# Fewer filler matmuls, small turns taken together, the slots' sum one slot later, and a combine in even blocks

## The chip, the core and the metric

The kernel runs on one NeuronCore of a Trainium2 chip. TensorE (PE in the profile, its weight loads PEld) does the matmuls, VectorE (DVE), ScalarE (ACT) and GpSimd (POOL) the work between them, and SyncE's queue (SPq) issues every DMA. Each engine takes its instructions in the order in which they were written; an engine that waits holds up all that stands behind it. The metric is the time of one execution on the device, in microseconds (us), as a median over runs.

## What is computed

Two things in a row, cut here to what matters. First a recurrence over time with a decaying state, for 4 batches and 8 heads, 768 steps, 48 numbers per head:

```python
for t in range(S):
    cur = np.einsum('bhd,bhe->bhde', u[None] * kt, vt)
    y[:, :, t] = np.einsum('bhd,bhde->bhe', rt, state + cur)
    state = wt[:, :, :, None] * state + np.einsum('bhd,bhe->bhde', kt, vt)
```

Its output, x with 3072 rows (tokens) of 384, goes through a soft mixture of 8 experts with 4 slots each:

```python
logits = x @ phi
d = np.exp(logits - logits.max(0)); d /= d.sum(0)     # over the tokens
slot_input = d.T @ x                                  # 32 slots
slot_out[e] = np.maximum(slot_input[e] @ w1[e], 0.0) @ w2[e]
c = np.exp(logits - logits.max(1)); c /= c.sum(1)     # over the slots
return c @ slot_out
```

## The kernel before

The time axis is cut into 6 chunks of 128 steps. The main loop (L702) has 16 turns, n = 0 to 15, called slots here: slot n handles one pair of heads, and four of them (j = 0 to 3) make a batch. A seventeenth pass (n = 16) only ends the last pair. The order of all work is written by hand: nothing is moved by a scheduler, and every engine runs its part in the written order.

What a slot does, with the names that the change touches:

- DVE makes the running products of the decays for the packed inputs (units u, three per batch): `a_back` (L507) and `a_fwd` (L518) are scans over 774 columns, `a_k` (L515) and `a_r` (L524) multiply k and r by them. POOL makes the products r times k (`a_rk`, L502) in two buffers that alternate.
- PE turns k (`b_kn`, L538; ACT copies it out, L540 and L542), makes the chunk states (`b_u`, L571), the scores in two halves (`b_scores`, L549, into the two PSUM banks ap) and the bonus terms (`b_bonus`, L563, which read the buffer of `a_rk` and write the bank that the state scan reads).
- ACT copies each half of the scores out (`b_at`, L554) and POOL masks it (L556). DVE scans the states (`b_state`, L580). POOL multiplies v by the bonus (`b_av`, L596).
- One slot later PE adds up the result of the pair, `c_inter` (L605) and `c_av` (L614, its second half reads the second half of the masked scores), and `c_evac` takes it out of the two banks y: DVE for one head (L625), ACT and POOL for the other (L627, L628).
- Two slots later `l_turn` turns x (L73, into the banks y; ACT copies it out, L640), and `l_mm` (L77) multiplies by phi. One batch later the soft part follows: `s_max` and `s_exp` (L96), then in the slot j = 3 `s_dturn` (L103, ACT copy L105) and `s_rows` (L128, ACT copy L130), which share one bank tp[1] but use other columns of it, and `s_mm` (L110), the sum over tokens, into that bank too. `s_acc` (L122, L124) and `s_sum` take it out on DVE. `s_rows_exp` and `s_norm` make the weights for the combine.

`keep_warm` (L664) issues matmuls of a constant with 512 columns whose result nobody reads, called fillers here. The table `warm` (L666) says how many stand at five places of each of the first four slots.

After the loop the end starts at L831: the last turns and logits, the soft part of the last batch, `up_proj` (L186), `up_relu`, `turn`, then `down_proj` (L222) in three groups of output columns (160, 160 and 64). `mix` (L242) makes the combine c @ slot_out of one column group in blocks, four banks at a time, DVE and ACT copy them out (L247), and SP writes them (L249). It is a generator: `down_proj` calls its next step after each of its 8 inner rounds through the list `steps` (L904). The weights come by DMA throughout, 512 KB or 640 KB at a time.

Of the kernel before, what the change touches and what calls it, by code (L numbers as in the profile page):

```python
# [49 lines left out]
def rwkv_soft_moe(ctx: ExitStack, tc: tile.TileContext, wc, krc, vc, cst, w1, w2, out):  # L50
# [183 lines left out]
    def mix(cT, S4, cg, o, banks):  # L234
        lo, hi = COLS[cg]
        wd = hi - lo
        per = min(6, 512 // wd)
        for i0 in range(0, 6, per):
            ops = [banks[r][:, 0:per * wd].rearrange("p (i d) -> p i d", d=wd) for r in range(4)]
            for i in range(per):  # L240
                for r in range(4):
                    nc.tensor.matmul(out=ops[r][:, i, :], lhsT=cT[32 * r:32 * r + 32, i0 + i, :],  # L242
                                     rhs=S4[32 * r:32 * r + 32, lo:hi], start=True, stop=True)
            og = o[i0 // per][:, 0:4 * per * wd]
            for r in range(4):
                dst = og.rearrange("p (i r d) -> p i r d", r=4, d=wd)[:, :, r, :]
                (nc.vector.tensor_copy if r % 2 == 0 else nc.scalar.copy)(out=dst, in_=ops[r])  # L247
            yield
            nc.sync.dma_start(out=out[:, NT * lo + 4 * i0 * wd:NT * lo + 4 * (i0 + per) * wd],  # L249
                              in_=og)  # L250
# [379 lines left out]
    def l_turn(n, split=False):  # L630
        b, g = divmod(n, NG)
        kt = g - 1
        for t in range(C):
            l_turn_mm(xb[b % 2], t, kt, yb[t // 3][:, (t % 3) * P:(t % 3 + 1) * P])
        xT = xTs[kt % 2].rearrange("p (f c) t -> p f (c t)", f=2)
        if split:
            nc.scalar.copy(out=xT[:, 0], in_=yb[0][:, 0:384])
            nc.vector.tensor_copy(out=xT[:, 1], in_=yb[1][:, 0:384])
        else:
            nc.scalar.copy(out=xT, in_=ypp[:, :, 0:384])  # L640
# [25 lines left out]
    warm = {0: (0, 8, 8, 8, 8), 1: (4, 4, 4, 4, 4), 2: (4, 3, 3, 3, 3), 3: (2, 2, 2, 2, 2)}  # L666
# [23 lines left out]
    keep_warm(28, yb[0])  # L690
# [11 lines left out]
    for n in range(NIT + 1):  # L702
# [44 lines left out]
        if n == NIT:  # L747
            s_rows_exp(qs[b - 2])
            s_norm(b - 2, qs[b - 2])

        fill = warm.get(n, (0,) * 5)
        if live:
            keep_warm(fill[0], tp[1])
            b_kn(n)
        keep_warm(fill[1], yb[0])
# [4 lines left out]
        if live:  # L760
            b_u(n)
            keep_warm(fill[2], ap[0])
# [3 lines left out]
            b_bonus(n)  # L766
# [82 lines left out]
    s_acc(lb, q, sp)  # L849
    m_slots(q, yb[0][:, 0:KT * NS].rearrange("p (k s) -> p k s", s=NS))  # L850
# [47 lines left out]
    stage = [[wa[2], wa[3]], [wa[4], wa[5]], [wa[6]]]  # L898
# [5 lines left out]
    def steps(gen):  # L904
        return [lambda: next(gen, None)] * 7
# [92 lines left out]
```

## Time and profile before

| what | value |
|---|---|
| median of 3 runs | 235.68 us (233.25 to 236.63) |
| the profiled execution, its own time | 233.78 us |
| its span, first to last instruction | 232.1 us |
| mean granted clock of TensorE | 0.919 |
| instructions | 7909 |
| busy PE, DVE, POOL, ACT | 83%, 48%, 38%, 36% of the span |
| read from HBM, written | 44.44 MB, 4.72 MB |

The profiled execution took 1.9 us less than the median of the runs. The start of slot n is taken as the first L538 of that slot: slot 1 starts at 21.76, slot 4 at 49.12, slot 7 at 72.63, slot 8 at 85.95, slot 12 at 126.10 and slot 15 at 149.50 us. A row of the chain of waits or of the timeline has the start, the length, the engine and the line; in square brackets stands how long the engine had been idle and whose work ended that. A row of the windows view has a stretch, its length, the busy time of each engine with its number of instructions, and at its end the granted clock of TensorE, the share of DMA and its GB/s.

### The profile page before, as it was taken

How to read it: one execution, taken by the hardware profiler on the slowest of the kernel's cores; microseconds unless marked ns; L12 is line 12 of the kernel's file. 1: busy time of each engine (PE TensorE's matmuls, PEld its weight loads, DVE VectorE, ACT ScalarE, POOL GpSimd, SP SyncE). 2: the span in 40 equal slices, each digit the busy share in tenths (PEclk: the TensorE clock that was granted, in tenths of full speed). 3: DMA queues.
4: the chain of work that ended last, by engine and by line, in shares of the span. 5: the costliest groups of instructions: out<-in, count | busy, mean ns of one | idle time of the engine just before them, and what ended most of it. 6: DMA issues, size and time to landing. Idle time of an engine off the chain costs nothing.

```text
span 232.1 us, 7909 instructions
## 1 busy us (share of the span) xinstructions
PE 192.0 (83%) x3450; PEld 133.3 (57%) x3450; DVE 111.9 (48%) x181; ACT 84.1 (36%) x185; POOL 88.0 (38%) x130
## 2 busy tenths in 40 slices
PE   7999999988899589699858969968767987979620
PEld 2455866767787448668644867856323222757420
DVE  5888518537837648562765763423132141033410
ACT  3323233364467344435634537454120011112310
POOL 4347174385576354663645565537000000000000
PEclk9999999999999979959997999999765699999985
DMA  6987294996885895959089735993860089007470
GB/s 178 351 266 226 84 305 161 360 326 153 343 273 212 293 377 92 392 134 370 4 304 367 176 131 152 402 412 93 316 192 0 0 318 380 10 3 315 196 287 35
DMA packets 14922, 52.13 MB, mean 225 GB/s; under 512 B 1952, under 2 KB 2720, under 8 KB 14880
## 3 DMA queue, kind: packets, MB, share of 16 engines
q1 hardware_dynamic: 14880, 51.55, 63.6%
q8 instruction: 29, 0.48, 0.9%
q14 instruction: 13, 0.11, 0.2%
HBM read 44.44 MB, written 4.72 MB: 212 GB/s over the span
## 4 chain that ended last, share of the span: by engine, by line
PE 59%; DVE 15%; POOL 8%; ACT 5%; issue 4%; DMA 2%; SPq 1%; DVEq 0%; ACTq 0%; POOLq 0%
PE y L664 6%; PE G L186 6%; PE y L614 6%; PE ap L549 5%; PE y L222 5%; PE tp L563 4%; PE y L73 4%; PE tp L77 4%; PE tp L110 3%; POOL blkat L556 3%; POOL blka L502 3%; PE ap L664 3%; DVE Traw L580 2%; PE y L605 2%; DMA wa<-in_w_dram 2%
## 5 line engine op out<-in xcount | busy, mean ns | idle before, releaser
L556 POOL TENSOR_SCALAR_AFFINE_SELECT blkat<-blkat 128x768 f32<-128x768 f32 x32 | 27.6, 864 | 19.9 <-ACT blkat L554 17.1
L554 ACT COPY blkat<-ap 128x768 f32<-128x768 f32 x32 | 25.5, 798 | 23.5 <-PE ap L549 22.5
L614 PE MATMUL y<-v,blkat 128*64 128x48 f32 x768 | 27.2, 224 | 5.2 <-POOL blkat L556 5.2
L614 PEld LDWEIGHTS y<-v,blkat 128*64 128x64 f32 x768 | 24.3, 138 | 7.0 <-POOL blkat L556 6.1
L549 PE MATMUL ap<-krb 48*128 48x128 f32 x288 | 23.5, 297 | 0.0
L625 DVE TENSOR_TENSOR x<-y,av 128x288 f32<-128x288 f32 x17 | 7.7, 456 | 31.3 <-PE y L614 31.0
L628 POOL TENSOR_TENSOR x<-x,av 128x288 f32<-128x288 f32 x15 | 12.0, 801 | 27.9 <-ACT x L627 27.9
L507 DVE TENSOR_TENSOR_SCAN G<-blkw,G 128x774 f32<-128x774 f32 (+1 forms) x13 | 21.3, 1642 | 1.5 <-DMA blkw<-in_wc_dram 1.2
L549 PEld LDWEIGHTS ap<-krb 48*128 48x128 f32 x288 | 18.8, 195 | 5.4 <-issue 2.5
L518 DVE TENSOR_TENSOR_SCAN G<-blkw,G 128x774 f32<-128x774 f32 (+1 forms) x13 | 21.4, 1649 | 0.4
L664 PE MATMUL y<-siT 128*128 128x512 bf16 x62 | 17.3, 427 | 1.6 <-DVE siT L683 1.6
L515 DVE TENSOR_TENSOR krb<-krb,G 128x774 f32<-128x774 f32 (+1 forms) x13 | 11.6, 892 | 14.5 <-POOL blka L502 14.5
L502 POOL TENSOR_TENSOR blka<-krb 128x768 f32<-128x768 f32 x11 | 17.1, 1553 | 2.5 <-DMA krb<-in_krc_dram 2.5
L627 ACT COPY x<-y 128x288 f32<-128x288 f32 x15 | 6.0, 401 | 32.4 <-DVE x L625 32.4
L664 PEld LDWEIGHTS <-siT 128*128 128x128 bf16 x106 | 9.9, 103 | 13.1 <-issue 3.8
L186 PE MATMUL G<-wa,siT 128*32 128x512 f32 x96 | 13.9, 713 | 1.4 <-ACT x L194 1.1
L596 POOL TENSOR_TENSOR av<-v,asb 128x576 f32<-128x576 f32 x12 | 14.1, 1176 | 0.0
L580 DVE TENSOR_TENSOR_SCAN Traw<-tp,blkm 112x288 f32<-112x288 f32 x16 | 12.1, 754 | 3.0 <-PE tp L571 3.0
L73 PE MATMUL y<-cst,x 128*128 128x128 f32 x72 | 11.6, 303 | 1.7 <-DVE x L625 1.7
L222 PE MATMUL y<-wa,x 128*32 128x160 f32 (+1 forms) x144 | 12.2, 274 | 0.7 <-issue 0.7
L524 DVE TENSOR_TENSOR krb<-krb,G 128x774 f32<-128x774 f32 (+1 forms) x13 | 11.6, 892 | 0.8 <-POOL blka L502 0.5
L563 PE MATMUL tp<-cst,blka 128*64 128x4 f32 x288 | 11.0, 205 | 1.1 <-DVE Traw L580 0.7
(146 smaller groups left out, 337.5 us busy)
## 6 DMA issues: line engine op xcount, KB each, us to landing
wa<-in_w_dram SPq DMA_DIRECT2D x24, 512.0 KB, 7.0
krb<-in_krc_dram SPq DMA_DIRECT2D x11, 774.5 KB, 5.8
v<-in_vc_dram SPq DMA_DIRECT2D x16, 288.0 KB, 5.6
blkw<-in_wc_dram SPq DMA_DIRECT2D x11, 387.0 KB, 3.4
wa<-in_w_dram SPq DMA_DIRECT2D x6, 640.0 KB, 5.6
out_dram<-wa SPq DMA_DIRECT2D x4, 960.0 KB, 3.9
krb<-in_w_dram SPq DMA_DIRECT2D x4, 640.0 KB, 8.5
blka<-krb SPq DMA_DIRECT2D x24, 96.8 KB, 2.9
```

The source lines that it names most:

```text
L73: nc.tensor.transpose(out=tp, in_=x[:, t, kt * P:(kt + 1) * P], identity=ident)
L186: nc.tensor.matmul(out=hp[32 * g:32 * g + NS, :], lhsT=siT[:, e * KT + kt, :], rhs=wts[e][:, kt * F + hf * 512:kt * F + hf * 512 + 512], s ...
L222: nc.tensor.matmul(out=so[32 * g:32 * g + NS, :], lhsT=hT[ft // 2][:, ft % 2, e, :], rhs=wts[E + e][:, FT * lo + ft * wd:FT * lo + (ft + 1 ...
L502: nc.gpsimd.tensor_tensor(out=rks[u % 2][:, c0:c0 + cn_], in0=k3, in1=r3, op=ALU.mult)
L507: nc.vector.tensor_tensor_scan(out=G[:, lo:hi][:, ::-1], data0=w[:, lo:hi][:, ::-1], data1=g_one.broadcast_to([P, hi - lo]), initial=1.0, ...
L518: nc.vector.tensor_tensor_scan(out=G[:, lo:hi], data0=ws[u % 2][:, lo:hi], data1=g_zero.broadcast_to([P, hi - lo]), initial=1.0, op0=ALU.m ...
L549: nc.tensor.matmul(out=ap[h][:, cc * P:(cc + 1) * P], lhsT=kt[64 * h:64 * h + D, c * PIT + 1:c * PIT + PIT], rhs=rt[64 * h:64 * h + D, c * ...
L554: nc.scalar.copy(out=ats[n % 2][hf].rearrange("p h c t -> p h (c t)"), in_=app[:, :, 0:384])
L556: nc.gpsimd.affine_select(out=at, in_=at, pattern=[[0, 6], [1, P]], compare_op=ALU.is_gt, fill=0.0, base=0, channel_multiplier=-1)
L563: nc.tensor.matmul(out=aP[p:p + 64, c, :], lhsT=rks[(NU * b + g) % 2][:, c, p:p + 64], rhs=ub[:, g, :], start=True, stop=True)
L614: nc.tensor.matmul(out=yb[h][p:p + 64, c * D:(c + 1) * D], lhsT=ats[n % 2][c // 3][:, h, c % 3, p:p + 64], rhs=vt[:, c, h, :], start=False ...
L664: nc.tensor.matmul(out=bank[:, 0:512], lhsT=zb[:, 0:P], rhs=zb, start=True, stop=True)
```

## The change

1. The table `warm` is gone. Fillers are left only in slot 0 (4, 4 and 8, beside 24 in place of 28 at the very start); slots 1 to 3 have none. At the end, between the last turns, logits and sums, new fillers stand: 4, 5, 3 and 4, into the bank that `up_proj` uses later.
2. `s_turns` does the turns of `s_dturn` and `s_rows` one behind the other, four matmuls, and then the two ACT copies.
3. `s_mm`, `s_acc` and `s_sum` move from the end of slot j = 3 into the next slot, j = 0, ahead of the bonus. For batch 2, whose next slot is n = 16, they stand there at its start.
4. `b_bonus` moves behind `l_mm`, `s_mm` or `s_turns` of its slot.
5. `l_turn` moves behind the second half of the scores, and takes the bank pair as an argument. At n = 16 and in the end it uses ap, and it stands ahead of `c_inter` and `c_av` there.
6. `s_exp` stands behind the second half of the scores.
7. `mix` makes blocks of three row groups in all three column groups (the last was one block of six), issues the write as soon as a block's copies are written, and `steps` leaves two rounds of `down_proj` between the first and the second block.

Line numbers of the changed kernel are a little higher (`b_scores` is L559 there, `b_kn` L548, `c_inter` L615, `c_av` L624, `b_u` L581, `b_bonus` L573, `s_mm` L120, the fillers L674).

On PE, at the seam of slots 7 and 8, this stands in the row before (names: tp1 is the bank tp[1], ap and y the bank pairs, dT and dN the exponentials and their turn, blka and krb the packed inputs):

```order
L103 MATMUL tp1_80<-cst_61,dT_993 128x96 x2
L128 MATMUL tp1_80<-cst_61,lt_107 128x96 x2
L73 MATMUL y_81<-cst_61,x1_98 128x128 x6
L549 MATMUL ap_78<-blka_93 128x128 x6
L110 MATMUL tp1_80<-x0_97,dN_1090 32x384 x6
L538 MATMUL tp1_80<-cst_61,krb1_92 128x112 x4
L538 MATMUL tp0_79<-cst_61,krb1_92 128x112
L605 MATMUL y_81<-Tc1_106,blka_93 64x48 x20
L614 MATMUL y_81<-v1_100,blkat_94 64x48 x24
L571 MATMUL tp0_79<-v2_101,blkm_95 48x48 x10
L549 MATMUL ap_78<-krb1_92 128x128 x6
L563 MATMUL tp0_79<-cst_61,blka_93 64x4 x12
```

In the changed kernel PE has there:

```order
L109 MATMUL tp1_80<-cst_61,dT_935 128x96 x2
L111 MATMUL tp1_80<-cst_61,lt_107 128x96 x2
L559 MATMUL ap_78<-blka_93 128x128 x6
L73 MATMUL y_81<-cst_61,x1_98 128x128 x6
L548 MATMUL tp1_80<-cst_61,krb1_92 128x112 x4
L548 MATMUL tp0_79<-cst_61,krb1_92 128x112
L615 MATMUL y_81<-Tc1_106,blka_93 64x48 x20
L624 MATMUL y_81<-v1_100,blkat_94 64x48 x24
L581 MATMUL tp0_79<-v2_101,blkm_95 48x48 x10
L559 MATMUL ap_78<-krb1_92 128x128 x6
L120 MATMUL tp1_80<-x0_97,dN_1026 32x384 x6
L573 MATMUL tp0_79<-cst_61,blka_93 64x4 x12
```

The sum over tokens (L110, now L120) has moved from ahead of the turn of k to just ahead of the bonus, and the turn of x has changed places with the second half of the scores.

At the end of the loop, from slot 15's small turns on, PE has this in the row before:

```order
L103 MATMUL tp1_80<-cst_61,dT_1961 128x96 x2
L128 MATMUL tp1_80<-cst_61,lt_107 128x96 x2
L73 MATMUL y_81<-cst_61,x1_98 128x128 x6
L549 MATMUL ap_78<-blka_93 128x128 x6
L110 MATMUL tp1_80<-x0_97,dN_2051 32x384 x6
L605 MATMUL y_81<-Tc1_106,blka_93 64x48 x20
L614 MATMUL y_81<-v0_99,blkat_94 64x48 x24
L73 MATMUL y_81<-cst_61,x1_98 128x128 x6
L77 MATMUL tp1_80<-blkm_95,cst_61 32x256 x6
L73 MATMUL y_81<-cst_61,x1_98 128x128 x6
L77 MATMUL tp1_80<-blkm_95,cst_61 32x256 x3
L148 MATMUL tp0_79<-cst_61,nM_64 96x96
```

And this in the changed kernel, up to the first of the new fillers:

```order
L109 MATMUL tp1_80<-cst_61,dT_1903 128x96 x2
L111 MATMUL tp1_80<-cst_61,lt_107 128x96 x2
L559 MATMUL ap_78<-blka_93 128x128 x6
L73 MATMUL y_81<-cst_61,x1_98 128x128 x6
L120 MATMUL tp0_79<-x0_97,dN_1987 32x384 x6
L73 MATMUL ap_78<-cst_61,x1_98 128x128 x6
L77 MATMUL tp1_80<-blkm_95,cst_61 32x256 x3
L615 MATMUL y_81<-Tc1_106,blka_93 64x48 x20
L624 MATMUL y_81<-v0_99,blkat_94 64x48 x24
L77 MATMUL tp1_80<-blkm_95,cst_61 32x256 x3
L674 LDWEIGHTS siT_67
L674 MATMUL G_77<-siT_67 128x512
```

One turn of x and half of the first logits now stand ahead of the last pair's result, in other banks, and fillers behind it.

The diff, cut to its core:

```diff
+    def s_turns(q, dp, ln):
+        for n in range(2):
+            nc.tensor.transpose(out=dp[:, n, 0:TG], in_=q["dT"][:, n, :], identity=ident[0:TG, 0:TG])
+        for n in range(2):
+            nc.tensor.transpose(out=ln[:, n, 0:TG], in_=q["lt"][:, n, :], identity=ident[0:TG, 0:TG])
+        q["dN"] = small.tile([P, 2, TG], F32, name="dN", bufs=1)
+        nc.scalar.copy(out=q["dN"], in_=dp[:, :, 0:TG])
+        q["ce"] = ce = small.tile([P, 2 * NTG, NS], F32, name="ce", bufs=1)
+        nc.scalar.copy(out=ce.rearrange("p (n j) s -> p n (j s)", n=2), in_=ln[:, :, 0:TG])
...
     def mix(cT, S4, cg, o, banks):
-        per = min(6, 512 // wd)
+        per = 3
         for i0 in range(0, 6, per):
-            ops = [banks[r][:, 0:per * wd].rearrange("p (i d) -> p i d", d=wd) for r in range(4)]
+            off = i0 * wd if 6 * wd <= 512 else 0
+            ops = [banks[r][:, off:off + per * wd].rearrange("p (i d) -> p i d", d=wd) for r in range(4)]
...
+            nc.sync.dma_start(out=out[:, NT * lo + 4 * i0 * wd:NT * lo + 4 * (i0 + per) * wd], in_=og)
             yield
-            nc.sync.dma_start(out=out[:, NT * lo + 4 * i0 * wd:NT * lo + 4 * (i0 + per) * wd],
-                              in_=og)
...
-    warm = {0: (0, 8, 8, 8, 8), 1: (4, 4, 4, 4, 4), 2: (4, 3, 3, 3, 3), 3: (2, 2, 2, 2, 2)}
...
-    keep_warm(28, yb[0])
+    keep_warm(24, yb[0])
...
         if n == NIT:
-            s_rows_exp(qs[b - 2])
-            s_norm(b - 2, qs[b - 2])
+            q = qs[b - 2]
+            sp0 = tp[0][0:TG, 0:DM]
+            s_mm(xb[b % 2], q, sp0)
+            l_turn(l, app)
+            l_mm(0, xTs[0], lpv, True, False)
+            s_acc(b - 2, q, sp0)
+            s_sum(b - 2, q)
+            s_rows_exp(q)
+            s_norm(b - 2, q)
...
         if live:
             b_u(n)
-            keep_warm(fill[2], ap[0])
+            if n == 0:
+                keep_warm(4, ap[0])
             b_scores(n, 0)
             b_at(n, 0)
             b_state(n)
-            b_bonus(n)
+        if j == 0 and b > 1 and live:
+            q = qs[b - 2]
+            s_mm(xb[b % 2], q, spv)
+            s_acc(b - 2, q, spv)
+            s_sum(b - 2, q)
...
         if soft and j == 3:
-            q = qs[sb_]
-            s_dturn(q, dpv)
-            s_rows(q, lnv)
+            s_turns(qs[sb_], dpv, lnv)
+        if live:
+            b_bonus(n)
...
-        keep_warm(fill[3], yb[1])
-        if l >= 0 and lj >= 1:
-            l_turn(l)
+        if live:
+            if n == 0:
+                keep_warm(4, ap[0])
+            b_scores(n, 1)
+            b_at(n, 1)
+            if n == 0:
+                keep_warm(8, yb[0])
+        if l >= 0 and lj >= 1 and live:
+            l_turn(l, ypp)
         if soft and j == 2:
             s_exp(sb_, q)
-        if live:
-            keep_warm(fill[4], ap[0])
-            b_scores(n, 1)
-            b_at(n, 1)
-        if soft and j == 3:
-            s_mm(xb[sb_ % 2], q, spv)
-            s_acc(sb_, q, spv)
-            s_sum(sb_, q)
...
-    l_mm(0, xTs[0], lpv, True, False)
+    warm_bank = Gp[:, 0:512]
     l_mm(1, xTs[1], lpv, False, False)
-    l_turn(NIT - 1, split=True)
+    keep_warm(4, warm_bank)
+    l_turn(NIT - 1, app, split=True)
+    keep_warm(5, warm_bank)
     l_mm(2, xTs[0], lpv, False, True)
+    keep_warm(3, warm_bank)
...
     s_acc(lb, q, sp)
+    keep_warm(4, warm_bank)
...
     def steps(gen):
-        return [lambda: next(gen, None)] * 7
+        return [lambda: next(gen, None), lambda: None, lambda: None, lambda: next(gen, None)]
```

More of the change, by code (lines that the diff above doesn't have):

```diff
@@ L628, in c_evac, with l_turn @@
                 nc.gpsimd.tensor_tensor(out=xh, in0=xh, in1=avs[n % 2][:, h], op=ALU.add)
-    def l_turn(n, split=False):
+    def l_turn(n, pp, split=False):
         b, g = divmod(n, NG)
@@ L633, in l_turn @@
         for t in range(C):
-            l_turn_mm(xb[b % 2], t, kt, yb[t // 3][:, (t % 3) * P:(t % 3 + 1) * P])
+            l_turn_mm(xb[b % 2], t, kt, pp[:, t // 3, (t % 3) * P:(t % 3 + 1) * P])
         xT = xTs[kt % 2].rearrange("p (f c) t -> p f (c t)", f=2)
         if split:
-            nc.scalar.copy(out=xT[:, 0], in_=yb[0][:, 0:384])
-            nc.vector.tensor_copy(out=xT[:, 1], in_=yb[1][:, 0:384])
+            nc.scalar.copy(out=xT[:, 0], in_=pp[:, 0, 0:384])
+            nc.vector.tensor_copy(out=xT[:, 1], in_=pp[:, 1, 0:384])
         else:
-            nc.scalar.copy(out=xT, in_=ypp[:, :, 0:384])
+            nc.scalar.copy(out=xT, in_=pp[:, :, 0:384])
     lpv = tp[1][0:TG, 0:2 * P].rearrange("p (n q) -> p n q", n=2)
@@ L747, in rwkv_soft_moe @@
         if n == NIT:
-            s_rows_exp(qs[b - 2])
-            s_norm(b - 2, qs[b - 2])
-        fill = warm.get(n, (0,) * 5)
+            q = qs[b - 2]
[7 more added lines that the diff above has]
+            s_norm(b - 2, q)
         if live:
-            keep_warm(fill[0], tp[1])
             b_kn(n)
-        keep_warm(fill[1], yb[0])
         if m >= 0:
@@ L803, in rwkv_soft_moe @@
             b_av(n)
-        keep_warm(fill[3], yb[1])
-        if l >= 0 and lj >= 1:
-            l_turn(l)
+        if live:
[7 more added lines that the diff above has]
+            l_turn(l, ypp)
         if soft and j == 2:
             s_exp(sb_, q)
-        if live:
-            keep_warm(fill[4], ap[0])
-            b_scores(n, 1)
-            b_at(n, 1)
-        if soft and j == 3:
-            s_mm(xb[sb_ % 2], q, spv)
-            s_acc(sb_, q, spv)
-            s_sum(sb_, q)
-        if j == 0 and 1 < b < B + 1 and live:
+        if j == 0 and 1 < b and live:
             s_rows_exp(qs[b - 2], nc.gpsimd)
-        if j == 1 and 1 < b < B + 1 and live:
+        if j == 1 and 1 < b:
             s_norm(b - 2, qs[b - 2], nc.gpsimd)
@@ L897, in rwkv_soft_moe @@
     mb = [ap[0], ap[1], tp[0], tp[1]]
-    stage = [[wa[2], wa[3]], [wa[4], wa[5]], [wa[6]]]
+    stage = [[wa[2], wa[3]], [wa[4], wa[5]], [wa[6], wa[7]]]
     def fin(cg):
```

## The prediction, made before the changed kernel ran

> **What bounds the kernel now.** I read the granted clock by slices, the chain of waits in order of time, then the stretches by slot. The clock first, in 40 slices of 5.8 us: low digits stand in the loop (slices 15, 18 and 22) and for some 20 us at its end.
>
> ```profile
> PEclk9999999999999979959997999999765699999985
> ```
>
> The chain runs through PE's fillers (L664) until slot 3. The windows view of L664 alone gives PE's busy time and the number of fillers; then three places of the chain.
>
> ```profile
> 10.30:21.70 11.40, 8.23 (x36) 3.28 (x36) 1.00 0.76 227
> 21.70:32.10 10.40, 5.03 (x22) 1.71 (x20) 1.00 0.56 178
> 32.10:41.50 9.40, 3.91 (x15) 1.03 (x14) 1.00 0.61 230
> 41.50:49.10 7.60, 2.57 (x9) 0.62 (x8) 1.00 1.01 387
> ...
> 18.36 1.73 PE ap L664 x8
> 24.00 1.53 PE y L614 x48
> 52.05 0.91 PE y L614 x24
> ```
>
> Eight fillers take 1.73 us: 0.216 each, and they stand on PE between real work. From slot 4 on there are none. There the chain goes from the bonus on PE through POOL back to PE, and at the seam of slots 7 and 8 through DVE, ACT and the small turns:
>
> ```profile
> 71.89 0.43 DVE lt L773
> ...
> 78.39 0.47 DVE x L625
> 79.17 0.80 ACT blkat L554
> 80.25 0.38 PE tp L128 x2
> 80.64 0.66 PE y L73 x6
> 81.29 1.25 PE ap L549 x12
> 82.54 2.71 PE tp L110 x12
> 85.34 0.55 DVE SI L122
> 85.97 0.68 PE tp L538 x5
> ...
> 90.30 0.87 PE tp L563 x24
> 91.16 0.82 PE y L73 x6
> 92.04 1.55 POOL blka L502
> 93.85 1.13 POOL av L596
> 94.98 0.82 POOL blkat L556
> ```
>
> After the loop PE is the chain, half of the time at half clock:
>
> ```profile
> 158.17 1.48 PE tp L110 x12
> 162.73 0.83 DVE x L625 x2
> 163.60 1.54 PE y L73 x6
> 165.14 1.96 PE tp L77 x12
> 169.12 0.67 PE tp L77 x6
> 172.26 2.78 PE ap L110 x12
> 178.50 5.35 PE G L186 x24
> 184.26 3.57 PE G L186 x32
> ```
>
> The same 12 rows of L110 took 1.48 us at 158 and 2.78 at 172. 24 rows of L186 took 5.35, and the next 32 only 3.57.
>
> **The change, part by part.** The sum is made against the profiled execution, 233.78 us (span 232.1 and 1.7 around it).
>
> *Fillers of slots 0 to 3.* In slot 0 the result of the pair cannot come as early as PE could start it. POOL holds the mask of the second half (L556) behind `a_rk` of unit 2, which waited for its DMA, and `b_av`:
>
> ```profile
> 18.77 1.55 POOL L502 TENSOR_TENSOR blka<-krb 128x768 f32<-128x768 f32 x1 [0.90 <-DMA krb<-in_krc_dram]
> 20.54 1.18 POOL L596 TENSOR_TENSOR av<-v,asb 128x576 f32<-128x576 f32 x1
> 21.88 0.86 POOL L556 TENSOR_SCALAR_AFFINE_SELECT blkat<-blkat 128x768 f32<-128x768 f32 x1 [0.16 <-ACT blkat L554]
> ```
>
> That DMA's issue does not move. So the mask comes right behind L596, ends at 22.6, and the first c_av ends half its length (0.75) later, at 23.35 instead of 24.00 + 1.53 = 25.53: 2.2 gained, with fewer fillers or many. From there to 52.05, where the second half of slot 4's c_av starts, PE now has 38 fillers, counted in the written order (12 of slot 1 behind its c_av, 16 of slot 2, 10 of slot 3). At 0.216 they are 8.2. The waits that come up in their place, by the same rows: in slot 2 the POOL chain of 1.55 + 1.13 + 0.82 from the bonus to c_av's second half is longer than PE's work beside it by 1.3, and in slot 3 DVE's two scans push L625, and so ACT's copy and the scores, 1.0 late. So 2.2 + 8.2 - 2.3 and 0.4 for a shorter wait ahead of 52.05: **-8.5**. Ends: -10.4 with no new wait, and -2 if POOL and DMA hold slots 1 to 3 where they are.
>
> *Clock in the loop.* It falls without any long gap. In slot 9 the window below has PE busy 1.84 of 3.41 us, its gaps under 1 us each, and behind it the slot's mean is 0.74; slot 9 takes 12.9 us, its twin slot 13 at full clock 10.0. So one fall costs up to 2.9.
>
> ```profile
> 95.28:98.69 3.41, 1.84 (x50) 1.67 (x52) 1.74 (x3) 1.69 (x5) 1.54 (x3) 1.00 1.01 394
> ...
> 92.80:105.70 12.90, 11.09 (x181) 8.66 (x179) 7.28 (x10) 5.05 (x12) 8.12 (x12) 0.74 0.80 278
> 132.90:142.90 10.00, 8.15 (x181) 6.57 (x179) 5.91 (x8) 4.84 (x12) 6.31 (x11) 1.00 0.39 115
> ```
>
> In the changed kernel c_av's second half in slot 1 waits for that mask while PE has nothing else for some 2.8 us; with half a chance of a fall there (+1.45) and half a chance that slot 9's goes (-1.45) the likeliest net is **0**, between -2.9 and +5.8 (two falls more). The Trainium skill's page "TensorE: Matmul & The Clock Gate" (HAM oscillation) lets the clock fall only for an idle gap over about 3.4 us. By that rule slot 1 would not fall and slot 9's fall would be none; the window above disagrees, and the measurement decides. With the rule the sum would be 1.45 lower.
>
> *Seam of slots 7 and 8, and of 11 and 12.* The turn L128 waited for ACT's copy of L103's result, and ACT stood behind L554, L625 and so DVE's chain from 71.89. Now four matmuls go in one piece, but the second scores still need L554, so PE's wait shrinks and does not vanish. `l_mm` ahead of the bonus brings the start of DVE's chain 0.87 earlier (the bonus's length). So L554 ends at 79.97 - 0.87 = 79.1; scores 0.87 (L549 at full clock, the length that L563 has too), turn of x 0.82, and L538 starts at 80.8 instead of 85.97: -5.15. L110 comes back in slot 8, 1.48, and the wait for the mask there, 0.5. One more DMA, queue or POOL instruction is not issued. DVE's SI copy (0.55) now stands ahead of a later scan, which POOL's L502 holds anyway. Net -3.1, twice: **-6.2**. Ends: -7.4 (the waits in slots 9 and 13 shrink too) and 0 (rival 2).
>
> *Slot 15 to the logits.* One turn and half of the first logits go ahead of c_inter, where PE waited for L554 and for dN. Then L625 x2 still ends at 163.56; behind it came 1.54, 1.96, a turn and an evacuation until L77 at 169.12. Now the turn of the last pair alone stands behind it: 163.6, 0.5 of the four fillers in the way, 0.8 for the turn, 1.27 for its evacuation by ACT and then DVE, L77 at 166.2: **-2.9**. Ends -3.4 and -1.5 (if half clock stays).
>
> *Fillers at the end.* 4, 5, 3 and 4 lie where PE waits for L625, the evacuation, nM and SI; 16 x 0.216 = 3.5 fit in the waits but for those 0.5. What they are worth is the clock: L110 2.78 to 1.48, 24 rows of L186 from 5.35 to 24 x 3.57 / 32 = 2.68, small matmuls about 1.2: **-5.2**. Ends: -5.2 and 0.
>
> *Combine.* PE waits 0.98 ahead of the second block of the first group; two rounds of `down_proj` (8 rows each at 0.036, from 112 rows in 4.01) fill 0.58 of it. In the second group DVE's copies bind the next step: nothing. The last group in two blocks writes twice 384 KB for once 768 KB; the second block's matmuls wait for the first's copies in the same banks, so the last issue comes some 0.45 later, and the last write has half the bytes.
>
> ```profile
> 199.12 4.01 PE y L222 x112
> ...
> 208.80 0.41 PE L242 MATMUL ap<-x,blkw 32*128 32x160 f32 x2 [0.98 <-ACT wa L247]
> ...
> out_dram<-wa SPq DMA_DIRECT2D x4, 960.0 KB, 3.9
> ...
> out_dram<-wa SPq DMA_DIRECT2D x1, 768.0 KB, 5.3
> ```
>
> Its landing lies between half of 5.3 and the 3.9 of a larger write: 3.7 taken, so -1.6 + 0.45. Together **-1.8**; ends -2.8 and +0.5.
>
> Sum: -8.5 + 0 - 6.2 - 2.9 - 5.2 - 1.8 = -24.6, so 233.78 - 24.6 = 209.2. The median of the runs lies 1.9 above the profiled execution; with less than half of that added I forecast **210.0 us**.
>
> **Rivals.**
> 1. *The fillers at the end do not hold the clock.* For it: between them stand turns and waits, and windows only a little over half busy fell before. Against: in 163 to 173 PE would be busy over 70%. Then the last -5.2 goes, and 210.0 becomes 215.2. By the same clock page of the Trainium skill (Part 4, PE-mode transpose) turns do not count as activity, which makes this likelier; no run here shows it.
> 2. *POOL takes the loop's gain.* The bonus now comes 1.48 later in j = 0 and some 1.0 later in j = 1; `a_rk` (L502) waits for it, and c_av's second half waits for the 3.5 us of POOL behind it, where PE's work beside it is now 0.8 shorter (the turn or the sum that stood there). If that binds everywhere, the -6.2 goes: 216.2. Against: 91.98 to 95.80 was bound by it before, so part is paid already.
> 3. *Both*: 221.4.
> 4. *Slower: the clock stays low in the loop.* One mechanism: slots 1 to 3 without fillers start at half clock, and the loop, whose short matmuls hardly count, does not bring it back. Each slot so costs up to 2.9; from (24.6 + 4.7) / 2.9 = 10 slots on it is slower by over 2%; with all 15, 210.0 + 43.5 = 253. Against: slot 10 ran at full clock again behind slot 9's fall, with no filler near.
> 5. *The early gain is given back to DMA*: loads wait on DVE's scans, not on PE, and slots 1 to 3 keep their length but for 2: 216.5.
>
> **How the numbers follow.** My forecast 0.56, rival 1 0.16, rival 2 0.10, both 0.05, rival 5 0.08, rival 4 0.02, and 0.03 for mishaps within 2%. About 2% of this kernel's time, 4.7 us, is what a measurement can tell from no change. All but rival 4 and the last lie below 231: faster 0.95, same 0.03, slower 0.02. The forecast's own ends, with the clock's -2.9, the seams' -1.2 and the combine's -1.0, reach down to 205; upward rivals 1, 2 and 5 reach 216.5 and both 221.4. I take 203 to 220.
>
> **What would show it.** Slot 4's c_av second half near 43.5 instead of 52.05; slot 8's start some 5 earlier against slot 7's; L110 in slot 8 at 1.5; granted clock 1.00 from the logits through L186, its first 24 rows in about 2.7; a last write under 4. Slots 1 to 3 with the clock at 0.5, L186 still at 5.35 or c_av's second half waiting over 1 us in slots 5, 6, 9 and 10 would make the forecast wrong.

## The result, and the profile after

| | before | changed |
|---|---|---|
| median of the runs | 234.47 us (231.16 to 236.63, 4 runs) | 214.74 us (213.28 to 224.57, 4 runs) |
| the profiled execution | 233.78 us, span 232.1 | 215.24 us, span 213.5 |
| mean granted clock in it | 0.919 | 0.922 |

The ratio is 0.9227, with a 95% interval from 0.9086 to 0.9367: faster by 6 to 9%. 210.0 had been forecast, 4.7 less than was measured; 214.74 lies in the range. One of the four executions of the changed kernel, the one of 224.57, was granted a mean clock of 0.862, the other three 0.908 to 0.922.

The granted clock by slices of the changed kernel. The end is now at full clock but for the last slice; the low digits stand early, in slices 5 to 7, 11, 12 and 16.

```profile
PEclk9999655999559996999999999999999999999995
```

The windows view cut at the places of which the prediction speaks: slots 0 to 3, slots 4 to 14, slot 15 to the last logits (the last L77), from there to `up_proj`, its first 24 rows, and the rest. First the kernel before, then the changed one. The last three numbers are the granted clock, the share of DMA and GB/s.

```profile
10.07:49.12 39.05, 38.92 (x617) 25.95 (x615) 23.36 (x25) 13.92 (x29) 18.65 (x28) 1.00 0.72 247
49.12:149.50 100.38, 86.57 (x1860) 69.29 (x1858) 61.46 (x79) 49.84 (x108) 57.42 (x81) 0.93 0.72 244
149.50:169.12 19.62, 14.72 (x273) 10.41 (x272) 5.74 (x15) 7.80 (x17) 7.23 (x10) 0.91 0.77 283
169.12:178.50 9.38, 6.69 (x30) 3.27 (x31) 2.67 (x11) 1.51 (x6) 0.00 (x0) 0.57 0.31 95
178.50:183.85 5.35, 5.35 (x25) 1.06 (x26) 0.06 (x1) 0.00 (x0) 0.00 (x0) 0.50 0.00 0
183.85:232.10 48.25, 31.30 (x624) 19.89 (x624) 11.70 (x37) 7.89 (x20) 0.00 (x0) 0.92 0.48 186
```

```profile
8.91:46.11 37.20, 30.93 (x553) 26.16 (x554) 24.42 (x27) 14.25 (x30) 18.65 (x28) 0.82 0.70 238
46.11:142.62 96.51, 85.22 (x1859) 72.32 (x1857) 61.90 (x80) 50.33 (x109) 57.41 (x81) 0.93 0.79 264
142.62:158.62 16.00, 14.92 (x282) 10.70 (x281) 5.00 (x13) 7.82 (x17) 7.33 (x10) 1.00 0.80 290
158.62:165.62 7.00, 5.70 (x37) 2.48 (x38) 2.67 (x11) 1.51 (x6) 0.00 (x0) 1.00 0.75 297
165.62:168.40 2.78, 2.78 (x25) 0.74 (x26) 0.06 (x1) 0.00 (x0) 0.00 (x0) 1.00 0.02 6
168.40:213.50 45.10, 31.65 (x625) 20.15 (x624) 11.91 (x39) 8.12 (x22) 0.00 (x0) 0.93 0.51 198
```

Slots 0 to 3 lost 64 instructions of PE and 8.0 us of its busy time, but only 1.85 us of length: the clock there went from 1.00 to 0.82. The 96.51 of slots 4 to 14 are 3.87 less than before at the same mean clock. From slot 15 on every stretch came out about as forecast or shorter. The six differences and the first slot's earlier start (1.16) make the 18.6 by which the spans differ: 1.16 + 1.85 + 3.87 + 3.62 + 2.38 + 2.57 + 3.15.

What PE waited for between 30 and 140 us (us in total, times, the longest), first in the kernel before, then in the changed one:

```profile
PE tp L128 <- ACT dN L105: 5.1, 2, 2.6
PE y L614 <- POOL blkat L556: 4.1, 6, 1.1
```

```profile
PE ap L559 <- ACT blkat L564: 3.9, 4, 1.8
PE y L615 <- ACT blkm L650: 3.6, 8, 0.6
```

The wait for `dN` in the kernel before is its wait at the seams. In the changed kernel the wait there stands ahead of the second scores (first line); the prediction expected it to shrink and not to vanish. The wait for POOL's mask, 4.1 before, is down to 0.2. The wait of L615 is new, and no term had it: the turn of x now stands right ahead of the next slot's `c_inter` (L615), which writes the same two banks y, so PE waits there for ACT's copy of the turn (L650).

### The profile page after: what moved, and what is told of

Its sections match the earlier page's. It is cut to its first block, busy times and chain, and to the rows that moved or that the text cites. A ratio compares the mean times of both kernels' runs of the same rounds, so it can differ in the third digit from the quotient of the medians.

```text
span 213.5 us, 7814 instructions
## 1 busy us (share of the span) xinstructions
PE 178.5 (84%) x3397; PEld 135.5 (63%) x3400; DVE 111.6 (52%) x183; ACT 84.5 (40%) x187; POOL 88.1 (41%) x130
## 4 chain that ended last, share of the span: by engine, by line
PE 54%; DVE 14%; POOL 10%; ACT 7%; DMA 6%; issue 5%; SPq 1%; ACTq 0%; DVEq 0%; POOLq 0%
PE ap L559 10%; PE y L624 9%; DMA krb<-in_krc_dram 6%; PE G L196 5%; PE y L232 5%; DVE G L517 4%; PE y L615 4%; PE tp L581 3%; PE tp L77 3%; POOL blkat L566 3%; POOL av L606 3%; POOL blka L512 3%; PE tp L573 3%; ACT blkat L564 2%; DVE G L528 2%
## 5 line engine op out<-in xcount | busy, mean ns | idle before, releaser
L624 PE MATMUL y<-v,blkat 128*64 128x48 f32 x768 | 30.0, 238 | 4.1 <-POOL blkat L566 3.7
L564 ACT COPY blkat<-ap 128x768 f32<-128x768 f32 x32 | 25.6, 800 | 19.0 <-PE ap L559 17.7
L624 PEld LDWEIGHTS y<-v,blkat 128*64 128x64 f32 x768 | 27.2, 151 | 5.7 <-POOL blkat L566 4.2
L559 PE MATMUL ap<-krb 48*128 48x128 f32 x288 | 25.8, 315 | 1.1 <-issue 1.0
L559 PEld LDWEIGHTS ap<-krb 48*128 48x128 f32 x288 | 20.7, 210 | 3.1 <-issue 2.0
L517 DVE TENSOR_TENSOR_SCAN G<-blkw,G 128x774 f32<-128x774 f32 (+1 forms) x13 | 21.4, 1643 | 1.6 <-DMA blkw<-in_wc_dram 1.3
L525 DVE TENSOR_TENSOR krb<-krb,G 128x774 f32<-128x774 f32 (+1 forms) x13 | 11.6, 891 | 12.6 <-POOL blka L512 12.6
L573 PEld LDWEIGHTS tp<-cst,blka 128*64 128x64 f32 x288 | 10.2, 145 | 6.8 <-issue 5.0
L581 PE MATMUL tp<-v,blkm 128*48 128x48 f32 x320 | 11.2, 222 | 2.6 <-ACT blkm L552 2.6
L573 PE MATMUL tp<-cst,blka 128*64 128x4 f32 x288 | 11.2, 205 | 2.4 <-DVE Traw L590 1.4
L615 PE MATMUL y<-Tc,krb 48*64 48x48 f32 x480 | 10.6, 236 | 2.4 <-ACT blkm L650 2.4
L196 PE MATMUL G<-wa,siT 128*32 128x512 f32 x96 | 11.3, 597 | 1.4 <-ACT x L204 1.1
L615 PEld LDWEIGHTS y<-Tc,krb 48*64 48x64 f32 x480 | 9.1, 148 | 4.8 <-ACT blkm L650 3.8
```

Source lines behind the costliest of these rows:

```text
L196: nc.tensor.matmul(out=hp[32 * g:32 * g + NS, :], lhsT=siT[:, e * KT + kt, :], rhs=wts[e][:, kt * F + hf * 512:kt * F + hf * 512 + 512], s ...
L517: nc.vector.tensor_tensor_scan(out=G[:, lo:hi][:, ::-1], data0=w[:, lo:hi][:, ::-1], data1=g_one.broadcast_to([P, hi - lo]), initial=1.0, ...
L559: nc.tensor.matmul(out=ap[h][:, cc * P:(cc + 1) * P], lhsT=kt[64 * h:64 * h + D, c * PIT + 1:c * PIT + PIT], rhs=rt[64 * h:64 * h + D, c * ...
L564: nc.scalar.copy(out=ats[n % 2][hf].rearrange("p h c t -> p h (c t)"), in_=app[:, :, 0:384])
L573: nc.tensor.matmul(out=aP[p:p + 64, c, :], lhsT=rks[(NU * b + g) % 2][:, c, p:p + 64], rhs=ub[:, g, :], start=True, stop=True)
L615: nc.tensor.matmul(out=yb[h][p:p + 64, c * D:(c + 1) * D], lhsT=rt[64 * h:64 * h + D, c * PIT + p:c * PIT + p + 64], rhs=T[64 * h:64 * h + ...
```

## The experiments

Four kernels ran beside each other in each of three groups, each group on one chip with its own runs of the kernel before. A time follows the clock that its execution was granted: of the kernel before, one with a mean clock of 0.836 took 246.59 us and one at 0.945 took 227.88. So medians are compared inside a group, and stretches at clock 1.00 with each other.

### Fillers in the wait of slot 1

```diff
-    def c_av(n):
+    def c_av(n, fill=0):
...
         for c in range(C):
+            if c == 3 and fill:
+                keep_warm(fill, ap[0])
...
-            c_av(m)
+            c_av(m, 15 if n == 1 else 0)
```

> The changed kernel with 15 more fillers in slot 1, between the two halves of c_av, where PE waited 3.48 us for POOL's mask; they cost 15 x 0.216 = 3.2 us inside that wait, so nothing. Theory 1 (slots 1 to 3 lose to the clock what the missing fillers give): the granted clock stays 1.00 from 23 to 37 us, slot 4 starts near 42 instead of 46.1, and the time falls from 214.7 by 3 to 6, to 209 to 212. Rival (the new order holds slots 1 to 6 up, not the clock): the clock stays up, slot 7 starts within 1.5 us of its 74.4, and the time is 213 to 216.

211.73 us (208.52 to 215.65, 4 runs), ratio 0.9137 [0.884, 0.9434]. First what happens there in the changed kernel, from its chain of waits (start, length, work): the load of `krb` lands late, POOL takes its steps, and PE comes out of the wait of 3.48 us at half clock: 1.52 for 24 rows that take 0.91 at full clock.

```profile
10.38 9.13 DMA krb<-in_krc_dram
...
19.67 1.55 POOL blka L512
...
21.48 1.13 POOL av L606
22.61 0.82 POOL blkat L566
...
23.48 1.52 PE y L624 x24
```

With the fillers (timeline of PE):

```profile
19.84 3.41 PE L676 MATMUL ap<-siT 128*128 128x512 bf16 x14
23.19 0.91 PE L626 MATMUL y<-v,blkat 128*64 128x48 f32 x24
...
31.07 0.91 PE L626 MATMUL y<-v,blkat 128*64 128x48 f32 x24 [1.57 <-POOL blkat L566]
...
32.35 1.23 PE L559 MATMUL ap<-krb 48*128 48x128 f32 x12
```

The fall behind slot 1's wait is gone (0.91), and the next wait, 1.57 us in slot 2, has one behind it (1.23 for 12 rows that take 0.94 at full clock). One covered wait hands the fall on to the next: slot 4 starts at 46.18, where the changed kernel had 46.11 and theory 1 had put it near 42. Two limits of this run: its load landed earlier, so the mask was ready at 21.97, and the fillers, which end at 23.25, held c_av's second half up by 1.2 us. And the interval of its ratio covers that of the changed kernel, 0.9227, so no difference in time is shown.

### The turn of x ahead of the second scores again

```diff
+        if l >= 0 and lj >= 1 and live:
+            l_turn(l, ypp)
         if live:
             b_scores(n, 1)
             b_at(n, 1)
-        if l >= 0 and lj >= 1 and live:
-            l_turn(l, ypp)
```

> The changed kernel with the turn of x ahead of the second scores again, as before the change, and all else kept. Theory (the moved turn made a wait of its own: c_inter writes the banks y, which ACT's copy of the turn L650 still reads, 0.3 to 0.65 us in 8 slots): those waits go, second scores and masks come 0.8 later where POOL has the time, 214.7 falls by 1 to 3 us. Rival (the earlier mask is worth as much): c_av's second half waits for POOL instead, 0.5 to 0.8 in slots 5, 6, 9, 10, 13, and the time is 214 to 217.

209.03 us (205.97 to 211.61, 4 runs), ratio 0.9028 [0.8724, 0.9333]. The interval overlaps that of the changed kernel, which was not in this group, so neither theory nor rival is shown by the time. What PE waits for between 30 and 140 us in this version:

```profile
PE y L624 <- POOL blkat L566: 5.2, 6, 1.3
PE y L73 <- ACT x L637: 2.2, 2, 1.1
```

The wait of L615 is gone. In its place c_av's second half waits for POOL's mask, six times up to 1.3 us: rival 2's wait, which the moved turn had covered. So moving the turn trades 3.6 + 3.9 us of waits for 5.2 + 2.2: the same sum.

### The kernel before with fillers in slot 0 only

```diff
-    warm = {0: (0, 8, 8, 8, 8), 1: (4, 4, 4, 4, 4), 2: (4, 3, 3, 3, 3), 3: (2, 2, 2, 2, 2)}
+    warm = {0: (0, 8, 8, 8, 8)}
```

> The kernel before with nothing changed but the fillers of slots 1 to 3 taken out (46 fewer). Theory 1 (without them the clock falls): PE runs at half clock for 10 us or more in slots 1 to 4, the start of slot 7 moves by less than 3 us from 72.6, the time is 231 to 237. The prediction's step (their time is gained, -8.5 less what slot 0 gives): 225 to 228.

225.02 us (220.24 to 231.0, 4 runs) beside 233.8 (228.61 to 241.86, 7 runs): 8.8 less by the medians, about the prediction's term, but with ranges that overlap and no interval. In its profiled execution slots 0 to 3 took 36.58 us at a mean clock of 0.81, where the kernel before took 39.05 at 1.00: in the old order too the fillers' time is given back in part to the clock. How much of it, this run does not settle. At like clock the gain is about 7: 223.71 at 0.930 beside 230.63 at 0.929, and 226.34 at 0.915 beside 233.49 at 0.915.

### The changed kernel without the fillers at the end

```diff
-    keep_warm(4, warm_bank)
     l_turn(NIT - 1, app, split=True)
-    keep_warm(5, warm_bank)
     l_mm(2, xTs[0], lpv, False, True)
-    keep_warm(3, warm_bank)
...
-    keep_warm(4, warm_bank)
     m_slots(q, yb[0][:, 0:KT * NS].rearrange("p (k s) -> p k s", s=NS))
```

> The changed kernel without the 16 fillers of the end (4, 5, 3, 4), its order kept. The prediction's step (they hold the clock, worth 5.2): L120 of the end 2.8 instead of 1.5, the first 24 rows of up_proj 5.3 instead of 2.8, the time 218 to 221. Rival (the new order of the end alone keeps PE busy enough): those rows stay, and 214 to 215.5.

215.52 us (212.77 to 228.11, 6 runs), ratio 0.9386 [0.9194, 0.9577]. Its windows view, slots 0 to 3 and from the last logits to `up_proj`:

```profile
9.65:41.07 31.42, 25.57 (x553) 20.99 (x554) 23.33 (x25) 13.71 (x29) 18.57 (x28) 1.00 0.80 268
...
152.31:161.54 9.23, 6.45 (x30) 3.10 (x30) 2.67 (x11) 1.59 (x6) 0.00 (x0) 0.60 0.60 234
```

The second row says what the fillers at the end are for: 9.23 at clock 0.60 against 7.00 at 1.00. The median does not show it: 215.52 is near the 214.74 of the changed kernel, which was not in this group. The first row came unasked and says more. The code up to there is the changed kernel's, but in this execution the load landed earlier, PE waited 2.05 us in slot 1 and not 3.48, and the clock did not fall:

```profile
22.12 0.91 PE L624 MATMUL y<-v,blkat 128*64 128x48 f32 x24 [2.05 <-POOL blkat L566]
```

So slots 0 to 3 without the old fillers take 31.42 at full clock, 7.6 less than the 39.05 before. The changed kernel's profiled execution took 37.20, 5.8 more, and two things share this. From the start of slot 0 to c_av's second half in slot 1 it is 14.57 there and 12.47 here: 2.1 is the later load. From there to slot 4 it is 22.63 and 18.95: 3.7 is the fall of the clock.

### Fillers in the waits

```diff
-            c_av(m)
+            c_av(m, {1: 9, 2: 7}.get(n, 0))
...
         if live:
+            keep_warm({9: 4, 13: 4}.get(n, 0), ap[0])
             b_u(n)
...
+            keep_warm({3: 4, 7: 8, 11: 6}.get(n, 0), ap[0])
             b_scores(n, 1)
```

> The changed kernel with fillers only inside waits that its trace shows: 9 and 7 ahead of c_av's second half in slots 1 and 2, 4, 8 and 6 ahead of the second scores in slots 3, 7 and 11, 4 ahead of b_u in slots 9 and 13 (9 x 0.216 = 1.9 us where PE waited 2.1 to 3.5, and so on). The kernel computes the same. Theory A (the clock's falls behind these waits are what ate the gain in the loop): the low stretches 23-37, 53-64 and 81-85 go but for the middle one, whose wait is another; the loop is some 8 us shorter and the time is near 205 on a chip where the kernel before takes 234. Rival (the falls come by themselves, wherever PE is below some share): the low stretches move elsewhere and the time stays within 2 us of the changed kernel's, 211 to 215.

209.77 us (208.5 to 211.24, 6 runs), 3.6 less than the changed kernel in the same group (213.36), with clocks of 0.955 to 0.978 against 0.907 to 0.929; the time lies between theory A's and the rival's. The low stretches of slots 1 to 5 are gone in its profiled execution. The fillers at the seams were badly placed, as the timeline shows in slot 11:

```profile
107.83 2.72 PE L676 MATMUL ap<-siT 128*128 128x512 bf16 x6 [2.18 <-ACT blkat L564]
```

They write a bank that ACT is still copying out, so they stand behind the wait that they were to fill, and the clock falls in it (6 rows in 2.72; 1.3 at full clock, at 0.216 each).

### The turn of x back, and fillers in the waits that are left

```diff
+        if l >= 0 and lj >= 1 and live:
+            keep_warm({7: 4, 11: 4}.get(n, 0), yb[1])
+            l_turn(l, ypp)
         if live:
             b_scores(n, 1)
...
-            c_av(m)
+            c_av(m, {1: 9, 2: 7, 4: 5, 5: 2, 8: 6, 12: 6}.get(n, 0))
...
+            keep_warm({9: 4, 13: 4}.get(n, 0), ap[0])
             b_u(n)
```

> The turn of x ahead of the second scores again, as before, and fillers in the waits which that version's trace shows (9, 7, 5, 2, 6, 6 ahead of c_av's second half in slots 1, 2, 4, 5, 8, 12, 4 ahead of the turn in slots 7 and 11, 4 ahead of b_u in slots 9 and 13). The kernel computes the same. Theory A: no stretch at half clock in the loop, PE's waits for ACT's copy of the turn gone, time near 202. Rival: waits move from ACT's copy to POOL's mask and the falls go elsewhere: 207 to 211, as without the fillers.

206.18 us (205.32 to 214.4, 6 runs), 7.2 less than the changed kernel in the same group, 4 above theory A and just below the rival. No stretch of the loop is at half clock in its profiled execution. It was run once more as the base of the third group:

> The best version so far (turn of x ahead of the second scores, fillers in the waits that are left) once more, as the kernel that the three others of this group change in one thing. Theory: 206 with the loop at full clock, ratio near 0.88. Rival (its first result was luck of the clock): 209 to 211.

206.25 us (205.2 to 209.33, 6 runs), ratio 0.8983 [0.887, 0.9096]. This is the fastest version found, ahead of both kernels. Its windows view, slots 0 to 3, slots 4 to 14, and slot 15 to the last logits:

```profile
8.73:40.31 31.58, 29.63 (x571) 22.28 (x569) 24.26 (x26) 14.24 (x30) 17.91 (x27) 1.00 0.79 265
40.31:132.87 92.56, 88.69 (x1894) 69.86 (x1893) 62.02 (x80) 50.45 (x109) 58.14 (x82) 1.00 0.82 283
132.87:147.94 15.07, 14.94 (x282) 10.56 (x280) 4.99 (x13) 7.53 (x17) 7.38 (x10) 1.00 0.82 296
```

The whole loop is at full clock in this execution; three of the twelve of this version had a mean clock of 0.937 to 0.955 and took 209.33 to 214.4. Against the changed kernel's stretches it is 5.6 + 3.95 + 0.9 = 10.5 shorter, with 53 PE instructions more. Most of this is the loop's clock, as expected; in the 10.5 are also the later load of the changed kernel's profiled execution (2.1) and two pauses of PE in it (1.0 each, last section). The fillers of slots 7 and 11 again stand behind their wait, so a little is left there (not tried).

### The changed kernel again

> The changed kernel once more, on the same chip as the others of this group, to compare with. Theory: 214 where the kernel before takes 234, ratio 0.92, with low clock in stretches that differ from execution to execution (the wait in slot 1 between 2.1 and 3.5 us by the landing of a load).

213.36 us (211.85 to 214.35, 6 runs) beside 236.39 (227.88 to 246.59, 11 runs). The clock falls at 24.1, 51.4 and 106.1 us in the loop, where the first profile had it fall at 23.0, 53.7 and 81.0: as often, twice in the same slots and once in another.

### The old fillers of slots 1 to 3 in the changed kernel

```diff
+        fill = {1: (4, 4, 4, 4, 4), 2: (4, 3, 3, 3, 3), 3: (2, 2, 2, 2, 2)}.get(n, (0,) * 5)
         if live:
+            keep_warm(fill[0], tp[1])
             b_kn(n)
+        keep_warm(fill[1], yb[0])
...
+            keep_warm(4 if n == 0 else fill[2], ap[0])
             b_scores(n, 0)
...
+        keep_warm(fill[3], yb[1])
+            keep_warm(4 if n == 0 else fill[4], ap[0])
             b_scores(n, 1)
```

> The changed kernel with the old fillers of slots 1 to 3 put back at their old places (46 of them; slot 0 as changed). The kernel computes the same. The prediction's theory (fillers are work on the chain): slots 1 to 3 take some 6 to 8 us longer, 222 in all. Rival (fillers hold the clock, and without them it falls in slots 1 and 2 for 6 us): the clock is 1.00 until slot 4 and the time is within 2 us of the changed kernel's.

214.74 us (210.78 to 220.85, 7 runs), only 1.4 more than the changed kernel in the same group, and the ranges overlap: that taking the old fillers out of slots 1 to 3 gained anything in the end is not shown. But the two reach the same time in different ways. Slots 0 to 3 here:

```profile
8.54:47.98 39.44, 37.37 (x600) 25.34 (x601) 24.81 (x27) 14.31 (x30) 19.38 (x29) 0.96 0.77 267
```

39.44 against 31.58 with well placed fillers: the old ones are 8 us of work. In return six of the seven executions had clocks of 0.937 to 0.972, where the changed kernel had 0.907 to 0.929. At equal clock this version took 210.78 to 214.74 in four executions (0.968 to 0.972), the version with fillers in the waits 209.31 to 210.99 in three (0.969 to 0.971). At a lower clock there is one pair to compare: 220.85 at 0.916 here, 212.56 at 0.917 in the changed kernel.

### The old combine in the best version

```diff
-        per = 3
+        per = min(6, 512 // wd)
...
-            nc.sync.dma_start(out=out[:, NT * lo + 4 * i0 * wd:NT * lo + 4 * (i0 + per) * wd], in_=og)
             yield
+            nc.sync.dma_start(out=out[:, NT * lo + 4 * i0 * wd:NT * lo + 4 * (i0 + per) * wd], in_=og)
...
-        return [lambda: next(gen, None), lambda: None, lambda: None, lambda: next(gen, None)]
+        return [lambda: next(gen, None)] * 7
```

> The best version with the combine of the kernel before (blocks as before, a block's steps one after the other, the write a step after its copies, one last write of 768 KB). The kernel computes the same. The prediction's theory: 1.8 us slower than the best version (0.58 from a wait of PE ahead of the second block, 1.2 from the last write). Rival (up_proj's end to the end of the span fell by about 3 in the changed kernel, so the spread blocks are worth more): 3 us. Third: nothing, DMA sets the end either way.

209.15 us (208.12 to 212.36, 6 runs), ratio 0.9088 [0.9001, 0.9175]: 2.9 more than the base by the medians, and by the two profiled executions. The last copy of the combine (timeline), with the new combine and then with the old one:

```profile
197.06 0.33 ACT L258 COPY wa<-tp 128x192 f32<-128x192 f32 x1
```

```profile
197.27 0.48 ACT L257 COPY wa<-tp 128x384 f32<-128x384 f32 x1
```

From its end to the end of the span it is 203.4 - 197.39 = 6.0 us with the new combine and 206.3 - 197.75 = 8.55 with the old: 2.5 of the 2.9 is the last write, which has half the bytes.

### The old seam in the best version

The name of this run on record is that of another edit.

```diff
-            s_turns(qs[sb_], dpv, lnv)
-        if live:
-            b_bonus(n)
+            q = qs[sb_]
+            s_dturn(q, dpv)
+            s_rows(q, lnv)
...
+        if soft and j == 3:
+            s_mm(xb[sb_ % 2], q, spv)
+            s_acc(sb_, q, spv)
+            s_sum(sb_, q)
```

`b_bonus` goes back ahead of `l_mm`, and `s_mm`, `s_acc` and `s_sum` are taken out of the next slot.

> The best version with the scores' part of the seam as before: bonus ahead of l_mm, the two small turns in two pieces with ACT's copies between them, s_mm, s_acc and s_sum at the end of the same slot instead of a slot later. The kernel computes the same (and has its fillers at the end still, whatever the run is called). The prediction's theory: slots 7 and 11 get 5 us longer, slots 8 and 12 some 2 us shorter, 6.2 in all at full clock. Rival (with the clock held and POOL's mask waited for anyway, most of it is hidden): under 3 us.

217.58 us (216.12 to 219.86, 6 runs), ratio 0.9439 [0.9313, 0.9565]: 11.3 more than the base. The chain of waits in slot 7, with the old seam:

```profile
71.40 0.81 ACT blkat L564
72.20 0.23 ACT dN L105
...
72.48 0.38 PE tp L138 x2
72.86 0.86 PE y L676 x4
73.73 0.66 PE y L73 x6
74.38 0.87 PE ap L559 x12
75.25 1.45 PE tp L120 x12
...
76.80 0.55 DVE SI L132
```

and in the base:

```profile
69.85 0.41 ACT x L639
...
71.33 0.66 PE y L73 x6
71.98 0.87 PE ap L559 x12
72.85 0.63 PE tp L548 x5
```

As the prediction had it: the second small turn (L138) waits for ACT's L105, which stands behind L564, and the sum (L120) and its evacuation come ahead of the next slot. Slots 7 and 8 together take 20.45 us against 17.60 and slots 9 and 10 take 16.65 against 16.13, all at full clock: 3.4 for one seam. The second seam costs 5.5 in slots 11 and 12, because the clock falls in its longer wait (3.77 us; low from 108.4 to 115.3), and slot 15 another 1.3.

### The best version without the fillers at the end

The edit is the one above, made in the best version.

> The best version without the 16 fillers at the end. The kernel computes the same. The prediction's theory: the clock falls to half between the logits and up_proj in every execution, and the time is 5.2 us longer. Rival (the new order of the end leaves PE busy enough, and the fall comes in some executions only): 0 to 2 us longer.

209.77 us (207.66 to 213.05, 6 runs), ratio 0.9087 [0.8957, 0.9218]: 3.5 more than the base by the medians; the ranges overlap. From the last logits to `up_proj`:

```profile
150.01:158.40 8.39, 5.50 (x30) 2.84 (x30) 2.67 (x11) 1.51 (x6) 0.00 (x0) 0.72 0.67 263
```

8.39 at 0.72 against 7.01 at 1.00 in the base, and half clock on into `up_proj` until 164.

## Why the prediction was right, and where it was off

The direction, the size within 5 us and the places were right. That the number came so near is in part luck: the clock and a later load made the profiled execution 7.1 us longer than the sum has it, and the start of slot 0, slot 15 and the combine, all better than forecast, took back 3.3. By the terms of its sum, for the two profiled executions:

| term | predicted | measured | from |
|---|---|---|---|
| fillers of slots 0 to 3, at full clock | -8.5 | -7.6 | 31.42 against 39.05 |
| later load in slot 1 | none | +2.1 | 14.57 against 12.47 |
| clock in the loop | 0 (-2.9 to +5.8) | +5.0 | below |
| seams and slots 4 to 14, at full clock | -6.2 | -5.2 | -3.87 less 1.3 of clock |
| slot 15 to the logits | -2.9 | -3.6 | 16.00 against 19.62 |
| end fillers (and order) to `up_proj`'s 24th row | -5.2 | -4.95 | 9.78 against 14.73 |
| combine and the rest | -1.8 | -3.15 | 45.10 against 48.25 |
| start of slot 0 | none | -1.2 | 8.91 against 10.07 |

**The clock in the loop is the term that was furthest off.** The prediction put it at a net of 0, half a chance of a fall in slot 1 against half a chance that slot 9's goes, at most 2.9 for each fall. Slot 1's fall came and cost 3.7, since the clock stayed low for four windows and not one. A second one, from 53.7 to 64, made slots 4 and 5 21.4 us long; they took 16.0 in the run with the old fillers at full clock: 5.4, of which 1.0 is a pause of PE in slot 4. Slots 7 and 8 lost 1.0 (18.05 against 17.06 in the changed kernel's other execution). That is 10.1. The falls of the kernel before cost 0.8 in slot 7 and 1.3 in slot 11 (13.3 and 13.8; such a slot took 12.5 at full clock in the run with fillers in slot 0 only) and 3.0 in slot 9 (13.0 against 10.0 in slot 13): 5.1. Net +5.0, near the upper end of this term's range. One of the prediction's own signs of being wrong so came true: most of slots 1 and 2 ran at clock 0.5, from 23.0 to 36.7. That the falls come from the waits that the change uncovered is shown by filling them: the time fell by 7.2 with the turn of x back, and that loop then ran at 1.00, and by 3.6 without, with one fall left in the loop.

**The fillers** were sized right as work on the chain, 7.6 at full clock. The second half of slot 4's c_av, put at 43.5, started at 44.0 in the execution without a fall, and at 48.9 in the changed kernel's own profile. Whether the change kept any of it is not shown: the same kernel with the old fillers was within 1.4. The prediction priced the fillers as work and their absence as waits, but their absence as clock only by an even chance of one short fall. It also took the load in slot 1 as fixed and put the start of c_av's second half there at 22.6; it was 22.1 in the one execution and 23.5 in the other.

**The seams** were right in mechanism and size: 3.4 for one, measured by undoing it, where 3.1 had been put. Missed was that `c_inter` waits for ACT's copy of the turn (3.6 in all); it stands for the waits on POOL's mask that are gone (4.1), so the sum stayed near. What lacks of the 6.2 is 1.0, as much as PE's pause of 0.99 in slot 10. Rival 2's waits did not come in the changed kernel, where c_av's second half waited 0.2 in all from 30 to 140 us; they came only with the turn of x put back.

**Slot 15** and **the end** came out as forecast. Rival 1 fell: the clock is 1.00 from the logits through L186. But without the 16 fillers the time is 3.5 longer by the medians, not 5.2; the rest of the 4.95 would be the new order's own.

**The combine** was undersized: 2.9 by undoing it, 3.15 by the stretches. The last write's half was put at 1.6 less 0.45 for a later last issue; it was worth 2.5, and the last copy ended no later.

**Rival 4** was right that the clock falls without fillers, but the loop did bring it back, within one to four windows each time in the changed kernel; its point of decision, 10 slots at low clock, was not reached: there were some five. **Rival 5** came in small: at full clock slots 0 to 3 are near as short as forecast, but DMA sets how long slot 1's wait is (2.05 to 3.48 us), and its later load cost the profiled execution 2.1.

## What to carry over

Fillers that only stand between work cost their full length, and fillers inside a wait cost nothing, as long as they end before it does, and hold the clock: take out the first only together with putting in the second, and write them to a bank that nobody is still reading, or they queue behind the wait. When work is taken off the engine whose clock falls in its waits, price the stretch twice, once at full clock and once with a fall behind each wait that comes into the open. The last write of this kernel was paid in full, so make its bytes few.

## What the runs showed of the hardware

The clock moves on a grid. In eleven profiled executions every fall and rise between 10 and 208 us lies within 0.13 us of multiples of 3.41 us, with an offset that differs from execution to execution. Cut along that grid, the changed kernel and then the run without end fillers around slot 1 (the second number behind the stretch is PE's busy time):

```profile
19.64:23.05 3.41, 0.36 (x14) 0.23 (x9) 1.77 (x2) 0.00 (x0) 3.38 (x5) 0.99 0.95 318
23.05:26.46 3.41, 2.98 (x50) 2.89 (x52) 1.97 (x3) 0.40 (x1) 0.68 (x2) 0.50 0.36 140
...
33.29:36.70 3.41, 3.41 (x66) 3.32 (x64) 0.79 (x2) 0.40 (x1) 0.06 (x1) 0.51 1.01 399
36.70:40.12 3.42, 3.27 (x75) 2.79 (x73) 3.35 (x4) 2.28 (x5) 2.56 (x4) 1.00 0.03 10
```

```profile
17.74:21.15 3.41, 2.33 (x71) 1.93 (x69) 2.99 (x4) 0.62 (x2) 2.86 (x5) 1.00 0.72 161
21.15:24.56 3.41, 2.38 (x62) 2.14 (x62) 2.93 (x4) 0.51 (x2) 1.30 (x3) 1.00 0.92 351
```

In the first the wait fills one window (busy 0.36 of 3.41) and the clock is low in the next. In the second a wait of 2.05 us is split by the grid, 2.33 and 2.38 busy, and nothing falls. Of the windows at full clock after 17 us, all 17 with PE busy 51% or less were followed by a fall; of those between 52 and 80% some fell and most did not, and none above 80% fell. So where a wait of some 2 us lies on the grid has a part in whether the clock falls, and this fits that one kernel has its falls in other slots each time. It is not all. In slot 2 the run with fillers in slot 1 and the run without end fillers have the same wait, 1.57 and 1.58 us, each inside one window with PE busy 1.84:

```profile
29.48:32.89 3.41, 1.84 (x54) 1.77 (x54) 0.77 (x2) 0.28 (x1) 1.67 (x3) 0.99 1.01 393
```

```profile
27.97:31.39 3.42, 1.84 (x62) 1.66 (x58) 0.33 (x1) 0.16 (x2) 2.12 (x4) 1.00 0.99 369
```

Behind the first the clock fell, behind the second it did not; what tells them apart is open. The Trainium skill's page "TensorE: Matmul & The Clock Gate" (Part 1) has a window of 3413 ns that runs freely; these traces, with 3.41 us, agree. It asks for an idle window for the fall; here a half busy one sufficed.

The way back is longer than the way down, and it is open why. After the fall at 23.05 PE was busy 87 to 100% for four windows before the clock rose at 36.7, while the fall at 81.0 lasted one window and others two, three and five. By the same page of the Trainium skill (Part 1) a busy window of some 3.4 us brings the clock back; the first of these stretches had three that did not. What work counts as busy for it, no run here tells.

In a few places PE paused in the middle of one line with nothing that the profile names as its cause: 0.97 us at 53.1 in slot 4 and 0.99 in slot 10 of the changed kernel, 0.97 to 1.32 in four other runs. Each of these six begins 0.1 to 0.6 us behind the end of a transfer of 16 KB in the instruction queue (q8 of the profile's DMA queues). But the changed kernel has 28 such transfers and two pauses, and no experiment was made, so this is a trace to follow and not a cause.
